# A long convolution with a spectral mix on one core: first-transform tiles of one sequence each, and the two real classes packed into one

## The chip, the cores and the metric

The kernel runs on one core of a Trainium2 chip. The metric is the device time of one launch in microseconds. The core has five instruction streams that run side by side and meet at semaphores: TensorE (PE), VectorE (DVE), ScalarE (ACT), GpSimd (POOL) and SyncE (SP). POOL and SP issue the DMAs here, SP without conversion, POOL also with conversion from float32 to float16.

## The reference

```python
# x: (8, 5696, 128), h: (5696, 128), w_r, w_i: (64, 128, 128), w_ch: (128, 128)
Xf = rfft(x, n=2 * S, axis=1); Hf = rfft(h, n=2 * S, axis=0)       # S = 5696
v = irfft(Xf * Hf[None], n=2 * S, axis=1)[:, :S]                   # causal convolution by channel
X = rfft(v, axis=1)                                                # length S
Y = zeros_like(X)
Y[:, :64] = X[:, :64] @ (w_r + 1j * w_i)                           # per mode, over channels
u = v + irfft(Y, n=S, axis=1)
out = u + maximum(u @ w_ch, 0)                                     # float32
```

## The kernel before

A position is s = 64 q + p, with q of 0 to 88 and p of 0 to 63. The padded transform of length 11392 is done in two steps. The *first transform* runs over q, as a matmul with the constant F (`f1_sb`): 89 values, padded to 178, give 90 *classes* k = 0 to 89, as pairs of real and imaginary columns, so 180 columns. The *second transform* runs over p within a class, as matmuls with the strip M (`m_sb`) of the class. Classes 0 and 89 are real after the first transform. Behind the product with the filter's spectrum Hs, matmuls with W1 and W2 (`wc_sb`) undo the second transform; the result Z goes to a scratch tensor in DRAM, and matmuls with G add up the 64 modes from it on chip. In the last stage (the tail) S4 undoes the first transform, the mixed modes are added, and output tiles are made.

The eight sequences go in four *pairs* (`g_`); a pair is 256 columns of 128 channels each, sequence `b` 0 and 1. The work of a pair is:

- **Placement** (`x_place`, DVE): eight pieces of x, four of each sequence (`XC`), are copied to Xin, in rows of 130 so that a matmul can read one channel of all 64 p. For pair 0 they come from Xr, loaded at the start by POOL's queue; for pair 1 from Xh and Xt, for later ones from Xt, loaded by POOL's queue once a buffer is free.
- **First-transform tiles** (`a_tile`, 32 in a pair): four matmuls of 180 columns, one for each of four channels. The stationary operand is Xin's channel for 64 p of *both* sequences, so partitions 0 to 63 of a result belong to sequence 0 and 64 to 127 to sequence 1. One eviction, on DVE or ACT, writes 128 x 720 to As. A tile needs all eight pieces.
- **Ticks** (`tick`, four classes each; 23 in a pair, the last with two classes): `second` makes 16 matmuls of 128 columns with a contraction over 64 rows; the result is copied by ACT to Xs (`copied`), or read from PSUM for some; DVE multiplies it with Hs in both partition halves to U (`products`); two ticks later (`LC`) four W matmuls of 512 columns and two ACT copies to Zs follow, and three ticks later (`LM`) the matmuls with G (`modes`).

Tick 0 has a way of its own, as it stands right behind the first-transform tiles: its second transform is done for the first 116 channels (120 in pair 0; `DA`, `DF`) ahead of the last tiles' evictions, then for the rest, and DVE makes three products of it (`first_u`: sequence 0 without the last channels, all of sequence 1 from ACT's copy, the last channels of sequence 0). For the other pairs, six tiles of the next pair run within the last ticks of the pair before (`border`), the other 26 behind it.

The filter h goes the same way at the start: 16 tiles from Hp, evicted to Ah, then *filter ticks* (`filter_tick`), six of them (`LH`) among the first-transform tiles of pair 0, the rest in pair 0's ticks, six ticks ahead of their use. A filter tick ends with a cast to Hs and two DMAs on SP's queue that write the copy with the partition halves swapped; a product needs cast and copies. Ah's place is then loaded with G.

At the start PE runs 92 filler matmuls, then the h tiles with four fillers behind each (but the last), then 22 long fillers (`LONG`), all into PSUM banks that nobody reads. The first-transform tiles of pair 0 go to DVE and ACT by a written list (`SHARE`). POOL issues the loads of h, then x of pair 0, then M in six parts, then Xh, each in the order of the code.

Every queue is in program order; the class `Recorder` adds the waits, from what each step reads and writes.

## Time and profile before

| | |
|---|---|
| median of three runs | 372.22 us (372.2 to 372.45) |
| span of the profiled execution, first to last instruction | 370.1 us |
| median less span | 2.1 us |
| mean granted clock of TensorE | 0.999 |
| bytes moved by DMA | 103.94 MB |

The page gives the profiled execution by its span; no time of that execution outside the span is listed. In the page's groups a line can be that of a helper: L323 is every matmul, L311, L313, L315 and L317 every eviction, L320 every DMA, so groups are told apart by the tiles: ps<-F,Xin is a first-transform tile, ps<-As,M a second transform, ps<-Ah,M a filter tick, ps<-U,Wc the W matmuls, ps<-G,Zs the modes. "128x720" is partitions by elements.

### The profile page before, as it was taken

To read this page: it belongs to the slowest core of one execution; us is meant where nothing else is said; L and a number is where in the kernel's file an instruction comes from. 1 tells how busy PE (TensorE), PEld (TensorE's weight loads), DVE (VectorE), ACT (ScalarE), POOL (GpSimd) and SP (SyncE) were. 2 spreads that over 40 slices of the span, in tenths; PEclk is the share of its full clock that TensorE was granted. 3 is DMA by queue.
4 is the path that set the end of the run, shared out by engine and by line. 5 is a ranking of instruction groups with operands and counts; after the bars stand their busy time and mean duration, and the time that the engine had idled before them with its cause. 6 is when DMAs were issued, how large, how long until landed. Compare 5 with 4: busy or idle time off the path is not lost.

```text
span 370.1 us, 12455 instructions
## 1 busy us (share of the span) xinstructions
PE 354.7 (96%) x5350; PEld 276.5 (75%) x5350; DVE 291.8 (79%) x332; ACT 316.2 (85%) x499; POOL 75.2 (20%) x117
## 2 busy tenths in 40 slices
PE   7999899999999999999999999999999999999994
PEld 7878766667866668866668766668899888888873
DVE  3549899988999999989999988775357777756666
ACT  8559999999999999999999999995467777688885
POOL 8804012100833311823213001151000000000000
PEclk9999999999999999999999999999999999999999
DMA  7999979969999996999996999999999999999878
GB/s 139 209 271 382 249 165 292 232 198 283 93 140 213 263 258 186 132 160 215 263 278 128 171 310 363 342 345 388 381 410 386 413 410 408 418 399 376 326 291 349
DMA packets 87048, 103.94 MB, mean 281 GB/s; under 512 B 22730, under 2 KB 72522, under 8 KB 83438
## 3 DMA queue, kind: packets, MB, share of 16 engines
q1 hardware_dynamic: 64610, 81.33, 62.5%
q0 software_dynamic: 22384, 21.83, 35.4%
q8 instruction: 42, 0.69, 0.7%
q14 instruction: 12, 0.10, 0.1%
HBM read 70.61 MB, written 51.12 MB: 329 GB/s over the span
## 4 chain that ended last, share of the span: by engine, by line
PE 78%; ACT 10%; DMA 7%; DVE 3%; issue 1%; POOL 1%; DVEq 0%; POOLq 0%
PE ps L323 78%; ACT As L313 6%; DMA out_dram<-O 5%; DMA Hin<-in_h_dram 2%; ACT R L898 1%; DVE As L317 1%; ACT Xs L311 1%; DVE U L623 1%; POOL Hin L320 1%; ACT UT L311 1%; DVE O L899 0%; ACT Zs L311 0%; DVE Hp L438 0%; ACT C L313 0%; DVE Hs L315 0%
## 5 line engine op out<-in xcount | busy, mean ns | idle before, releaser
L652 DVE TENSOR_TENSOR U<-Xs,Hs 128x2048 f16<-128x2048 f16 (+1 forms) x72 | 85.8, 1197 | 12.1 <-ACT Xs L311 11.5
L323 PE MATMUL ps<-U,Wc 128*128 128x512 f16 (+1 forms) x368 | 93.8, 376 | 1.4 <-DVE U L623 1.4
L311 ACT CAST Xs<-ps 128x1024 f16<-128x1024 f32 (+1 forms) x76 | 75.0, 995 | 5.8 <-PE ps L323 3.1
L311 ACT CAST Zs<-ps 128x512 f16<-128x512 f32 (+1 forms) x132 | 70.1, 605 | 0.7
L899 DVE TENSOR_TENSOR O<-ps,R 128x512 f32<-128x512 f32 x81 | 52.4, 684 | 21.6 <-ACT R L898 11.4
L898 ACT ACTIVATE R<-ps 128x512 f32<-128x512 f32 (+1 forms) x92 | 50.5, 592 | 8.5 <-PE ps L323 8.4
L317 DVE TENSOR_SCALAR As<-ps 128x720 f16<-128x720 f32 x64 | 53.1, 879 | 4.8 <-PE ps L323 3.3
L323 PE MATMUL ps<-As,M 64*128 64x128 f16 (+3 forms) x1504 | 52.5, 214 | 2.4 <-ACT As L313 1.2
L313 ACT ACTIVATE As<-ps 128x720 f16<-128x720 f32 (+1 forms) x68 | 48.2, 771 | 5.0 <-PE ps L323 4.8
L323 PE MATMUL ps<-F,Xin 128*128 128x180 f16 x512 | 52.1, 249 | 0.1
L323 PE MATMUL ps<-WI,UT 128*128 128x256 f16 x360 | 50.8, 278 | 0.5 <-ACT UT L311 0.4
L311 ACT CAST UT<-ps 128x712 f16<-128x712 f32 x46 | 34.5, 752 | 19.4 <-PE ps L323 18.4
L323 PEld LDWEIGHTS ps<-U,Wc 128*128 128x128 f16 x368 | 29.1, 97 | 28.2 <-DVE U L623 1.9
L323 PEld LDWEIGHTS ps<-F,Xin 128*128 128x128 f16 x512 | 45.2, 155 | 6.7 <-DVE Xin L365 0.9
L323 PEld LDWEIGHTS ps<-As,M 64*128 64x128 f16 x1504 | 42.2, 94 | 8.7 <-ACT Xs L311 1.9
L323 PEld LDWEIGHTS ps<-WI,UT 128*128 128x128 f16 x360 | 38.9, 152 | 3.2 <-issue 1.8
L323 PE MATMUL ps<-IBs,C 128*128 128x356 f16 x128 | 39.2, 314 | 0.8 <-DVE O L899 0.7
L320 POOL DMA_DIRECT2D Xt<-in_x_dram x40 | 21.4, 540 | 76.5 <-PE ps L323 76.0
L323 PEld LDWEIGHTS ps<-G,Zs 128*128 128x128 f16 x512 | 26.1, 96 | 14.1 <-ACT Zs L311 0.2
L652 DVE TENSOR_TENSOR U<-ps,Hs 128x2048 f16<-128x2048 f32 (+1 forms) x16 | 35.5, 2216 | 0.0
L323 PE MATMUL ps<-G,Zs 128*128 128x128 f16 (+2 forms) x512 | 31.9, 192 | 0.1
L311 ACT CAST Zt<-ps 128x512 f16<-128x512 f32 x52 | 29.1, 659 | 0.0
(76 smaller groups left out, 479.4 us busy)
## 6 DMA issues: line engine op xcount, KB each, us to landing
out_dram<-O SPq DMA_DIRECT2D x39, 512.0 KB, 10.5
zscr<-Zs SPq DMA_DIRECT2D x62, 256.0 KB, 6.7
zscr<-Zt SPq DMA_DIRECT2D x26, 256.0 KB, 6.6
Xt<-in_x_dram POOLq DMA_DIRECT2D x20, 320.0 KB, 6.9
W<-wscr SPq DMA_DIRECT2D x4, 1024.0 KB, 8.5
ZT0a<-zscr SPq DMA_DIRECT2D x4, 1024.0 KB, 11.0
M<-cM POOLq DMA_DIRECT2D x5, 720.0 KB, 17.6
ZT1a<-zscr SPq DMA_DIRECT2D x3, 1024.0 KB, 11.1
```

What stands on the lines that cost most here:

```text
L311: R.add(e, lambda h_: h_.copy(dst, src), reads, writes, after=after)
L313: R.add(e, lambda h_: h_.activation(dst, src, COPY, scale=scale), reads, writes, after=after)
L317: R.add(e, lambda h_: h_.tensor_scalar_mul(dst, src, scale), reads, writes, after=after)
L320: R.add(eng, lambda h_: h_.dma_start(dst, src), reads, writes, ring=ring, after=after)
L323: R.add("tensor", lambda h_: h_.matmul(o, l, r, start=st, stop=sp), reads, writes)
L623: R.add("vector", lambda e: e.tensor_tensor(bass.AP(u_s[0], b * 512 + d0, [[2048, P], [1024, 2], [D, n], [1, d1 - d0]]), bass.AP(s_[0], s_ ...
L652: R.add("vector", lambda e: e.tensor_tensor(uv, src, hv, MULT), bk + [("h", t, 0), ("h", t, 1, 0), ("h", t, 1, J)], [("u", i)])
L898: R.add("scalar", lambda e: e.activation(rv, src_r, RELU), bk, [("r", i % NR)], after=once(("r", i % NR), G_ALL + XTT + [("y", 0), ("y", 1 ...
L899: R.add("vector", lambda e: e.tensor_tensor(ov, src_u, rv, ADD), bk + [("r", i % NR)], [key + (h_,)], after=once(key, old))
```

## The change

- **Layout of tiles.** Xin is laid out by channel halves, in rows of 66. The stationary operand of a tile's matmul is now channel d and channel d + 64 of *one* sequence: tiles 0 to 15 are sequence 0, tiles 16 to 31 sequence 1, and partitions 64 to 127 hold the second half of the channels, as h's tiles had it before. The second transform, products, W matmuls and Zs copies follow this order: 64 channels of two sequences where there were 128 channels of one. Hs is kept per tick, plain and swapped half side by side.
- **Pair 0's start.** x is loaded sequence after sequence (12 DMAs instead of 14). Sequence 0's four pieces are placed among the h tiles; its tiles then run, and sequence 1's pieces are placed among them, after tiles 1, 5, 9 and 13. The filter ticks follow tiles 19, 21, 23, 25, 27 and 29 (before: 11, 14, ... 26). Xh's loads wait for the last placement as before. Two fillers stand behind each h tile instead of four, and four long ones instead of 22; six of the h evictions go to DVE instead of two; `SHARE` is rewritten.
- **Tick 0.** The second transform of sequence 0 stands behind the last tile on PE, that of sequence 1 waits for the last evictions. There are two products, one for each sequence. The slot `DA`/`DF` split is gone.
- **89 classes.** The real classes 0 and 89 are the real and imaginary part of one. F has 178 columns, a tile's eviction 712 elements, and the last tick one class. In tick 0 this class has weights of its own, V1 and V2, so its W matmuls are eight instead of four with as many columns; in `modes` it is a full class with 128 columns (class 89 was one before, class 0 had two). The scratch tensor keeps 90 classes, and one load fills the unused rows at the start of pair 1.

```diff
-    NK = NQ + 1
+    NK = NQ
...
+    for b_ in range(2):
+        for c_ in range(XC):
+            first_rows(b_, c_)
+            if c_ == 0:
+                next_rows(b_)
+                last_row(b_)
...
-    ZSLOT, DA, DF = 6, 116, 120
+    ZSLOT = (6, 4)
...
-    WARM, LONG = 92, 22
+    WARM, LONG = 92, 4
...
-        for i in range(4 if j < 15 else 0):
+        for i in range(2 if j < 15 else 0):
...
-             eng="vector" if j in (3, 7) else "scalar")
-        if j % 2:
-            i = j // 2 % 2 * XC + j // 4
-            x_place(i, bass.AP(x_all, i * XB, [[RA, NQ], [D, XN], [1, D]]), XR[i])
+             eng="vector" if j in (2, 4, 6, 9, 11, 14) else "scalar")
+        if j % 4 == 3:
+            i = j // 4
+            x_place(i, bass.AP(x_all, i * XB, [[RA, NQ], [D, XN], [DH, 2], [1, DH]]), XR[i])
...
-    def a_tile(j, slots, eng=None):
+    def a_tile(j, slots, eng=None, first_pair=False):
+        b_ = j // 16
+        xin = XIN[b_ * XC:b_ * XC + XC] if first_pair else XIN
...
-               ap(x_sb, XW, 0, P, d, [[XS, 2 * J]]), f1_sb[:, :], True, True,
-               XIN + XZ + [("f1",)], [bank(t + i // 2)])
+               ap(x_sb, XW, 0, P, d // DH * 2 * XH + d % DH, [[HS, 2 * J]]), f1_sb[:, :], True, True,
+               xin + XZ + [("f1",)], [bank(t + i // 2)])
...
+                for dh in range(2):
+                    col = m_col(k, r) + dh * J
+                    mm(pv(sl + dh, bs[0] * 256 + i * DH, [[256, nb], [1, DH]]),
+                       ap(m_sb, MW, J * dh, J, col, [[1, P]]),
+                       ap(a_sb, AW, J * dh, J, (2 * k + r) * D + bs[0] * DH, [[1, nb * DH]]), r == 0, r == 1,
+                       rd + mtok(k), [bank(sl + dh)])
...
+            product(g_, t, (ps, sl[0], 4096), bk[0], (0,))
+            second(g_, 0, (1,))
+            evac(bass.AP(x_s[e], 256, [[1024, P], [512, 2], [1, n]]), pv(ZSLOT[1], 256, [[512, 2], [1, n]]), bk[1], [("xs", e)], eng="scalar")
+            product(g_, t, (x_s[e], 0, 1024), [("xs", e)], (1,))
...
-                for r in range(2):
-                    mm(pv(zb[b], 0, [[1, n * D]]), (W1, W2)[r], u_s[i][:, r * 1024 + b * 512:r * 1024 + b * 512 + n * D],
-                       r == 0, r == 1, [("u", i), ("wc",)], [bank(zb[b])])
+                for lo, hi, w_ in ((0, DH, (V1, V2)), (DH, n * DH, (W1, W2))) if s_ == 0 else ((0, n * DH, (W1, W2)),):
+                    for r in range(2):
+                        mm(pv(zb[b], lo, [[n * DH, 2], [1, hi - lo]]), w_[r],
+                           ap(u_s[i], 2048, 0, P, r * 1024 + b * 512 + lo, [[256, 2], [1, hi - lo]]),
+                           r == 0, r == 1, [("u", i), ("wc",)], [bank(zb[b])])
...
-    SHARE = [V if c_ == "V" else A for c_ in "VAVAAVAVAVAVAVAVAVAAVVAVAVAVAVA"]
+    SHARE = [V if c_ == "V" else A for c_ in "VAAVAAVAAVAAVAAVVAVAVAVVAVAVAVA"]
+    HTICK = [19, 21, 23, 25, 27, 29]
     for j in range(32):
-        a_tile(j, FOUR, "both" if j == 31 else SHARE[j])
...
+        a_tile(j, FOUR, "both" if j == 31 else SHARE[j], True)
+        for i in range(NXH if j == 15 else 0):
+            x_load(1, i, x_h[i], xtok(i), [t_ for r_ in XR for t_ in r_])
+        if j in HTICK:
...
+            filter_tick(HTICK.index(j), [h_, h_ + 1])
+        if j % 4 == 1 and j < 16:
+            i = XC + j // 4
+            x_place(i, bass.AP(x_all, i * XB, [[RA, NQ], [D, XN], [DH, 2], [1, DH]]), XR[i])
+    second(0, 0, (0,))
```

## The prediction

> **What bounds the kernel now.** I read the page's busy shares first, then the chain of waits in order of time, then the timelines of the stretches that the change touches.

> ```profile
> span 370.1 us, 12455 instructions
> PE 354.7 (96%) x5350; PEld 276.5 (75%) x5350; DVE 291.8 (79%) x332; ACT 316.2 (85%) x499; POOL 75.2 (20%) x117
> ...
> 17.25 10.56 PE ps L323 x102
> ...
> 49.37 25.23 PE ps L323 x529
> 74.60 20.63 PE ps L323 x300
> 95.26 7.47 ACT As L313 x11
> 102.78 0.37 PE ps L323 x8
> 103.17 0.59 ACT Xs L311
> 103.78 0.70 DVE U L623
> 104.58 0.27 DVE U L623
> 104.90 43.31 PE ps L323 x644
> ```

> The busy shares say TensorE, but the chain shows three regimes. Inside a pair PE runs without a gap (43.31 us in one piece). At each border between pairs evictions of first-transform tiles take over (7.47 us), followed by a handover: eight small matmuls, a copy, two small products, then PE again at 104.90. The third regime is the start, where the 10.56 us of PE are mostly fillers that cover the loading of x. The change touches all three. The span is 370.1 us and the median of the runs 372.22, so 2.1 us lie around the span; I make the sum as a difference and take it off the median.

> **The start: what the engines could do.**

> ```profile
> 11.98 2.37 DVE L438 COPY Hp<-Hin 89x4096 f16<-89x4096 f16 x2 [6.71 <-DMA Hin<-in_h_dram]
> 23.22 4.27 PE L323 MATMUL ps<-Hp,F 128*128 128x344 f16 x22
> 26.33 0.69 DVE L365 COPY Xin<-Xr 89x2048 f16<-89x2048 f16 x1 [0.81 <-DMA Xr<-in_x_dram]
> 40.95 2.19 DVE L317 TENSOR_SCALAR As<-ps 128x720 f16<-128x720 f32 x3 [0.40 <-PE ps L323]
> 91.70 10.85 DVE L317 TENSOR_SCALAR As<-ps 128x720 f16<-128x720 f32 x13
> ```

> Before, no tile of x can start until the eighth piece is placed at 26.33 + 0.69 = 27.0 us, and the last eviction ends at 40.95 + 2.19 = 43.1. The change puts sequence 0's four pieces first. h had landed at 11.98 and all of x at 26.33, so half the bytes, in order, are there at about 11.98 + 14.35/2 = 19.2.

> DVE then sets the pace. It is free of the Hp copies at 14.35, and one eviction costs (10.85 - 0.45)/12 = 0.87 us (the thirteenth is a half tile). In its new order it has 6 Ah evictions and 4 placements: 14.35 + 0.4 for the first tile + 6 x 0.87 + 4 x 0.69 = 22.7. The x of sequence 0 is there 3 us before. Tiles of sequence 0 start then. Up to the placement of the eighth piece DVE has 5 evictions and 4 placements after half a microsecond of PE: 22.7 + 0.5 + 5 x 0.87 + 4 x 0.69 = 30.3, by which time sequence 1 (26.33) has long landed. The rest is 9 evictions, one Hs cast (0.68, a row of it below) and a half: 9 x 0.87 + 0.68 + 0.45 = 9.0, so 39.3. ACT, with 10 + 7.5 tiles at 7.47/11 = 0.68 and 5 casts, is done no later.

> So the evictions end 3.8 us earlier. The fillers taken out (30 of 180 columns; 18 of the 22 long ones, 18 x 0.194 = 3.5 us by the second row) are worth nothing by themselves: PE then waits for DVE, under a microsecond around 22.

> **The start: what becomes late next.** The first products need Hs in both partition halves, and the swapped half comes by a DMA of SP's queue.

> ```profile
> 12.12 4.90 POOL L320 DMA_DIRECT2D M<-cM  x6
> DMA to landing us min/median/max: 16.5/18.2/21.7
> 27.60 4.15 POOL L320 DMA_DIRECT2D Xh<-in_x_dram  x8 [10.58 <-DVE Xin L365]
> Xh<-in_x_dram POOLq DMA_DIRECT2D x4, 320.0 KB, 12.9
> L320 SPq DMA_DIRECT2D Hs<-Hs x2: 555/571/587, 33.0 to 33.6; - x2
> DMA to landing us min/median/max: 6.6/7.0/7.4
> L320 SPq DMA_DIRECT2D Hs<-Hs x2: 461/529/597, 36.8 to 37.3; - x2
> DMA to landing us min/median/max: 9.5/9.6/9.8
> L320 SPq DMA_DIRECT2D Hs<-Hs x2: 542/568/595, 48.5 to 49.0; - x2
> DMA to landing us min/median/max: 2.0/2.0/2.0
> 43.43 1.16 DVE L623 TENSOR_TENSOR U<-ps,Hs 128x960 f16<-128x960 f32 x1 [0.29 <-PE ps L323]
> 47.42 1.23 DVE L652 TENSOR_TENSOR U<-Xs,Hs 128x2048 f16<-128x2048 f16 x1 [0.51 <-ACT Xs L311]
> 48.57 0.68 DVE L315 CAST Hs<-ps 128x512 f16<-128x512 f32 x1
> ```

> A swap takes 2.0 us when the queues are quiet and 7 to 10 us behind M and Xh, whose last piece lands near 27.60 + 4.15 + 12.9 = 44.7. Tick 0's pair lands at 33.6 + 7.4 = 41.0, its product ran at 43.43: 2.4 us to spare. Tick 2's lands at 37.3 + 9.5 = 46.8 and its product ran at 47.42: only 0.6 to spare. In the changed kernel the filter ticks follow tiles 19, 21, ... 29. By the same DVE count tick 0's cast ends at about 33.5 and tick 2's at 36.5, so the swaps are issued within half a microsecond of the old times. The queue ahead is the same M and Xh: Xh's eight issues move behind the later last placement, 27.0 to about 31, but M is on its way until 38 (issued up to 17.0, landing 16.5 to 21.7 us after issue, the second row), so the transfers close up.

> Hence tick 2's product goes from 47.42 to about 46.8, not to the 43.6 that the evictions allow. What stands behind it on DVE in order is the Hs cast of 48.57, and the filter matmuls of the next tick wait for that bank; from there DVE has one product, one cast and every other tick a placement, against a PE that is as full, so nothing is won back. The start gives 47.42 - 46.8 = **0.6 us**. Its bounds are -1 (swaps a microsecond and a half later than now) and 3.8 (swaps land as issued on a quiet queue).

> **Each border, three times.**

> ```profile
> 142.06 0.60 PE L323 MATMUL ps<-U,Wc 128*128 128x256 f16 x4
> 142.50 0.53 PE L323 MATMUL ps<-F,Xin 128*128 128x180 f16 x4
> ...
> 144.47 0.33 PE L323 MATMUL ps<-G,Zs 128*128 128x4 f16 x4
> 144.68 10.17 PE L323 MATMUL ps<-F,Xin 128*128 128x180 f16 x104
> 51.88 0.61 PE L323 MATMUL ps<-As,M 64*128 64x128 f16 x16
> 52.43 1.04 PE L323 MATMUL ps<-U,Wc 128*128 128x512 f16 x4
> ```

> With 89 classes the 23rd tick holds one class instead of two. Its four W matmuls of 256 columns fill 142.50 - 142.06 = 0.44 us and half that at best; I take 0.20 saved. Its second transform loses four of eight matmuls at (52.43 - 51.88)/16 = 0.034: 0.13. Its mode matmuls halve from 144.68 - 144.47 = 0.21: 0.10, of which I count nothing at the border, since evictions bind there already. First-transform tiles shrink from 720 to 712 elements; at 0.87 us for 720 an upper bound is 0.01 us each, 0.10 over 13 evictions in a row.

> The handover loses its second small product, with the gap ahead of it: PE went on at 104.90, the product before it ended at 103.78 + 0.70 = 104.48, and a wake-up costs 0.05. That gives 0.37. Against it stand eight more small matmuls ahead of the Xs copy (0.05, since the eight of 102.78 take 0.37 and most of that is latency). Product 0 of sequence 0 grows from 928 to 1024 elements but runs while PE and ACT do sequence 1. In tick 2, class 0 has its own weights V1, V2: eight W matmuls instead of four with the same columns. No row shows that form; between 0 and four issues of 0.034 I take 0.05. Sum: 0.20 + 0.13 + 0.10 + 0.37 - 0.05 - 0.05 = **0.70**, between 0.3 (only the handover) and 0.9; three times, 2.1.

> The last pair has no border; its last tick, with the mode matmuls and two Zs copies of half the length on the path to the mix, gives 0.2 + 0.1 + 0.05 = **0.35**.

> **Edits at nothing.** Products, Zs copies and placements keep their element counts but run in pieces of 64 per class and sequence. Rows for short runs: As evictions move runs of two at 0.87 us for 720, Hp copies runs of 32, 4096 elements in 1.2 us. Neither is dearer per element than a contiguous run, so I put 0 and keep the opposite as a rival. The zpad load (one DMA on SP, waiting for nothing, in pair 1) and the two rows fewer in S4b are covered; no wait moves with them. The tail's loads are asked for by PE's progress, so the tail moves as a block.

> **Sum.** 0.6 + 2.1 + 0.35 = 3.05: 372.22 - 3.05 = **369.2 us**.

> **The rivals.**

> (a) The swaps do not bind, because they land as early as they are needed: the start gives 3.8 less 0.2, the total 6.0, time 366.2. For it: filter casts from tick 3 on come over a microsecond earlier than now. Against it: 9.5 us at a still loaded queue.

> (b) The swaps land up to 2 us later than now, as the casts slip behind a slower DVE sequence: 369.2 + 0.6 to 2.2, say 370.5. It decides from tick 2's landing at 47.4.

> (c) Nothing measurable: the swaps slip by 3 us and the start gives back what the borders save, 372.2. Chance small; the casts would have to come near 40.

> (d) Slower, on DVE: the new patterns halve its rate. The two rows are windows of the trace: length, busy time of PE, weight loads, DVE, ACT and POOL, granted clock, DMA share, GB/s.

> ```profile
> 104.90:143.70 38.80, 38.80 (x591) 25.66 (x592) 36.66 (x32) 37.76 (x63) 8.33 (x16) 1.00 1.06 230
> 27.30:42.80 15.50, 14.96 (x226) 12.78 (x224) 13.68 (x17) 14.02 (x22) 4.15 (x8) 1.00 1.04 329
> ```

> A placement of 0.69 us would then cost up to 1.38; with some of it fixed I take 1.2, which is 0.53 more. Eight of them before 39.3 make 4.2, of which the 3.2 by which the start outran the swaps are free; eight in pair 0, where DVE sets the pace, make 4.2; in each later pair 4.2 less DVE's idle 38.80 - 36.66 = 2.1 of the first row. Together 1.0 + 4.2 + 2 x 2.1 = 9.4: 378.6. It is slower than before once a placement costs 0.4 us more (8 x 0.4 in pair 0 alone eat the 3.05). The Hp row speaks against it.

> (e) Slower, on PE's clock: fillers go while PE sits idle between 14 and 48 us. In the second row the granted clock is 1.00 in the stretch where evictions set the pace and PE is fed below its rate, so such gaps have cost nothing so far. The longest that I expect is an estimate of 2.3 us, from about 46.3, when the matmuls behind tick 1's product are through, to 48.6, the end of the cast behind tick 2's. Were PE at half rate from 22 to the end of the stage, 128 tile matmuls at twice 10.17/104 = 0.098 us and 96 filter matmuls at twice 0.034 make 31.6 us as an upper bound; as the 0.098 is itself set by evictions I take 24. The evictions then end at 46.7 instead of 43.1, and 372.22 + 3.6 - 2.45 = 373.4. It is slower than before if they end after 45.6.

> [...]

> **How the numbers follow.** My sum has 0.50, (a) 0.18, (b) 0.12, (c) 0.08, (d) 0.06, (e) 0.06. The measurement can tell 0.2%, 0.74 us, from no change. Faster: the sum, (a) and (b), 0.80; same: (c), 0.08; slower: (d) and (e), 0.12. The range runs from (a) at 366.2 to 371.9: it takes in (b) and the lower bounds of the borders (3 x 0.4 less) and leaves out (c), (d) and (e).

> **What would show it.** Right: sequence 0's first tile near 22.7 us, the last eviction of the first stage near 39, product 0 waiting for an Hs DMA at about 41 and tick 2's product at about 46.8; each pair 0.7 us shorter from one handover to the next; one handover product fewer. Wrong: tick 2's product before 46 (then (a)) or after 47.4 ((b)); a placement or product slower than now ((d)); a clock below 1.00 between 14 and 48 us ((e)).

## The result: slower, 383.58 us, and the profile after

| | before | changed |
|---|---|---|
| median of 6 runs each, same chip | 372.34 us | 383.58 us (380.96 to 385.46) |
| ratio | | 1.0288, 95% interval 1.025 to 1.0326 |
| profiled execution, span | 370.1 us | 382.7 us |

The prediction said 369.2 us. The profiled execution of the changed kernel took 385.46 us, 1.9 above the median, so the losses read from it below add up to 12.6 us of span and not to the 11.2 of the medians. First the page of the changed kernel: busy shares, the clock in 40 slices of 9.6 us, and pieces of its chain (start, length).

```profile
PE 353.0 (92%) x5290; PEld 272.7 (71%) x5290; DVE 291.6 (76%) x331; ACT 312.7 (82%) x496; POOL 73.5 (19%) x115
PEclk9999989999999999999999999998899999999998
38.27 11.56 DMA Hs<-Hs
108.32 0.70 DVE U L657
239.93 8.71 DMA zscr<-Zt
249.51 7.07 DMA zscr<-Zs
```

No engine has more work than before, PE has 1.7 us less. The clock dips twice, near 50 and from 258 to 277 (means of 0.82 and 0.85 over these slices), and DMAs stand in the chain where before there was PE; three of them are shown. By *handover* I mean below the end of DVE's product of sequence 1 in tick 0 of a pair. Before, the three were at 104.47, 157.46 and 210.48; now they are at 109.01, 162.04 and 215.45. So 4.5 us are lost ahead of the first, 0.4 in pairs 1 and 2, and 7.7 between the third and the end (159.6 us before, 167.3 now). Two things about this measure. Before, a second small product follows the one that ends the handover, and PE goes on 0.42 us behind it (104.90); now it goes on 0.14 behind it (109.16), so handovers favour the kernel before by 0.28. And the first handover scatters: two kernels below whose start is the one of before had it at 104.47 and 105.49, and four with the changed start (two of them with 48 small matmuls more) at 107.34 to 109.01. A difference of 1 us in it, in single traces, shows nothing.

**Start.** DVE's timeline of the changed kernel (start, length, in brackets the idle time before):

```profile
23.65 0.90 DVE L341 TENSOR_SCALAR As<-ps 128x712 f16<-128x712 f32 x1 [0.63 <-PE ps L347]
29.58 0.68 DVE L389 COPY Xin<-Xr 89x2048 f16<-89x2048 f16 x1
38.52 1.62 DVE L341 TENSOR_SCALAR As<-ps 128x712 f16<-128x712 f32 x2 [0.25 <-PE ps L347]
42.90 1.22 DVE L657 TENSOR_TENSOR U<-ps,Hs 128x1024 f16<-128x1024 f32 x1 [2.76 <-DMA Hs<-Hs]
49.49 1.22 DVE L657 TENSOR_TENSOR U<-Xs,Hs 128x2048 f16<-128x2048 f16 x1 [3.21 <-DMA Hs<-Hs]
```

Evictions and placements come within a microsecond of the forecast; the products do not. Swaps on SP's queue, then PE, then two windows (length; busy of PE, weight loads, DVE, ACT, POOL; clock, DMA share, GB/s):

```profile
36.47 2.40 SPq L344 DMA_DIRECT2D Hs<-Hs  x4
38.91 0.59 SPq L344 DMA_DIRECT2D G<-cG  x1
40.55 4.90 SPq L344 DMA_DIRECT2D Hs<-Hs  x4
49.26 1.10 SPq L344 DMA_DIRECT2D Hs<-Hs  x2
DMA to landing us min/median/max: 12.4/12.6/12.7
51.37 0.41 PE L347 MATMUL ps<-Ah,M 64*128 64x64 f16 x16 [3.01 <-DVE Hs L339]
48.00:52.00 4.00, 0.99 (x38) 0.82 (x37) 2.51 (x4) 0.90 (x2) 0.00 (x0) 1.00 0.45 141
52.00:56.00 4.00, 4.00 (x55) 2.44 (x49) 4.00 (x5) 2.39 (x4) 1.04 (x2) 0.57 0.92 164
```

Tick 2's swaps, issued at 36.47, land 12.6 us later (9.6 before). The ring `"s"` has eight semaphores, so the ninth swap waits on SP for the first to land: four issues take 4.90 us instead of 2.40, and the next two stand until 49.26. PE stands 3.01 us, and the mean clock of the window from 52 to 56 is 0.57.

**Tail.** S4b is the second part of the constant S4, `zscr` the scratch tensor, Zs and Zt are the buffers from which Z is stored to it, and ZT0a and ZT0b the tail's first loads of Z. SP's queue around the load of S4b, the kernel before (two rows), the changed one (three), then ACT and PE of the changed one:

```profile
224.35 1.35 SPq L320 DMA_DIRECT2D S4b<-cS  x1
228.94 0.45 SPq L320 DMA_DIRECT2D ZT0b<-zscr  x1
...
228.59 0.42 SPq L344 DMA_DIRECT2D S4b<-cS  x1
229.85 2.62 SPq L344 DMA_DIRECT2D zscr<-Zt  x2
233.24 6.64 SPq L344 DMA_DIRECT2D ZT0b<-zscr  x1
...
249.75 1.07 ACT L335 CAST Zs<-ps 128x512 f16<-128x512 f32 x2 [2.15 <-DMA zscr<-Zs]
256.66 1.41 ACT L335 CAST Zs<-ps 128x512 f16<-128x512 f32 x4 [2.60 <-DMA zscr<-Zs]
257.30 0.34 PE L347 MATMUL ps<-U,Wc 128*128 128x128 f16 x2 [2.37 <-ACT Zs L335]
```

Behind an S4b of 82 rows the issue of ZT0b takes 6.64 us instead of 0.45, stores of Z land late, ACT waits for their buffers, and PE for ACT.

### The profile page after: what moved, and what is told of

Read it like the earlier page. It is cut to its first block, busy times and chain, and to the rows that moved or that the text cites. A ratio compares the mean times of both kernels' runs of the same rounds, so it can differ in the third digit from the quotient of the medians.

```text
span 382.7 us, 12323 instructions
## 1 busy us (share of the span) xinstructions
PE 353.0 (92%) x5290; PEld 272.7 (71%) x5290; DVE 291.6 (76%) x331; ACT 312.7 (82%) x496; POOL 73.5 (19%) x115
## 4 chain that ended last, share of the span: by engine, by line
PE 63%; DMA 15%; ACT 11%; DVE 5%; issue 3%; POOL 1%; SPq 1%; DVEq 0%; POOLq 0%; ACTq 0%
PE ps L347 62%; ACT As L337 8%; DMA Hs<-Hs 4%; DMA Xt<-in_x_dram 4%; DMA Xr<-in_x_dram 3%; DMA zscr<-Zt 2%; DMA zscr<-Zs 2%; DVE As L341 2%; DVE Xin L389 1%; ACT Xs L335 1%; ACT R L928 1%; POOL Hin L344 1%; ACT Zs L335 1%; DVE Hs L339 1%; DVE U L657 1%
## 5 line engine op out<-in xcount | busy, mean ns | idle before, releaser
L657 DVE TENSOR_TENSOR U<-Xs,Hs 128x2048 f16<-128x2048 f16 (+2 forms) x76 | 87.7, 1160 | 20.2 <-ACT Xs L335 11.3
L347 PE MATMUL ps<-U,Wc 128*128 128x512 f16 (+2 forms) x384 | 94.2, 367 | 7.3 <-ACT Zs L335 4.2
L335 ACT CAST Xs<-ps 128x1024 f16<-128x1024 f32 (+2 forms) x76 | 74.5, 988 | 12.9 <-PE ps L347 11.0
L341 DVE TENSOR_SCALAR As<-ps 128x712 f16<-128x712 f32 (+1 forms) x63 | 52.2, 873 | 5.3 <-PE ps L347 4.1
L347 PE MATMUL ps<-F,Xin 128*128 128x178 f16 x512 | 52.2, 249 | 1.9 <-DVE Xin L389 1.3
L347 PE MATMUL ps<-As,M 64*128 64x128 f16 (+1 forms) x1488 | 50.7, 215 | 2.3 <-ACT As L337 2.3
L337 ACT ACTIVATE As<-ps 128x712 f16<-128x712 f32 (+1 forms) x69 | 48.2, 764 | 3.8 <-PE ps L347 3.6
L347 PEld LDWEIGHTS ps<-As,M 64*128 64x128 f16 x1488 | 40.8, 95 | 7.5 <-ACT As L337 2.8
L657 DVE TENSOR_TENSOR U<-ps,Hs 128x2048 f16<-128x2048 f32 (+2 forms) x20 | 39.8, 1990 | 2.8 <-DMA Hs<-Hs 2.8
L347 PE MATMUL ps<-IBs,C 128*128 128x356 f16 x128 | 40.4, 325 | 0.1
L347 PE MATMUL ps<-G,Zs 128*128 128x128 f16 (+2 forms) x504 | 31.6, 194 | 0.2 <-ACT Zs L335 0.2
```

The lines of the kernel that those rows point to most:

```text
L335: R.add(e, lambda h_: h_.copy(dst, src), reads, writes, after=after)
L337: R.add(e, lambda h_: h_.activation(dst, src, COPY, scale=scale), reads, writes, after=after)
L341: R.add(e, lambda h_: h_.tensor_scalar_mul(dst, src, scale), reads, writes, after=after)
L347: R.add("tensor", lambda h_: h_.matmul(o, l, r, start=st, stop=sp), reads, writes)
L657: R.add("vector", lambda e: e.tensor_tensor(uv, sv, hv, MULT), bk + [("h", t, 0), ("h", t, 1, 0), ("h", t, 1, J)], [("u", i)])
```

## The experiments

Theory: S4b's 82 rows (tail) and the late swaps with their ring (start). Rivals: the fillers taken out; something else in the tail. All medians stand against the kernel before on the same chip (372.1 to 372.8 in the four sets); differences between kernels of different sets are taken as they stand, and can be off by these 0.7.

**S4b with 84 rows.**

```diff
-        n = PB + RB if part else P      # 82 rows
+        n = PB + RL if part else P      # 84 rows, the last two zero
```

> Changed kernel with one edit: the load of S4b takes 84 rows again (32 of padding, 50 of data, 2 rows of zeros) instead of 82. Theory (82 rows clog a few transfer engines, and the zscr stores, the ZT loads and the last Zs casts queue behind them, until PE's gaps drop its clock): the zscr stores issued near 229.9 and 231.8 land in about 7 us instead of 12 to 14, the 2.15 and 2.60 us of ACT idle near 249.8 and 256.7 go, the clock stays at 1.00 from 250 to 277, and the kernel takes 376 us, 7 to 8 less than the changed one (383.6). Rival (the tail is late for another reason, the longer rows of ZT0b or the zpad rows): the gaps stay, 383. Rival (the fillers taken out let the clock fall): no change in the tail, 383.

377.68 us, 1.0143 (1.0116 to 1.017), 5.9 less than the changed kernel. ZT0b's issue is short again, ACT's waits for stores are gone. It is 1.7 more than forecast: in the tail the clock still dips once (0.65 from 260 to 264), behind a gap that comes up below.

```profile
231.03 0.43 SPq L344 DMA_DIRECT2D ZT0b<-zscr  x1
```

**The reverse, in the kernel before:** the same bytes in two DMAs, of 82 and of 2 rows.

> Kernel before with one edit: S4b is loaded in two pieces, of 82 rows and of 2 rows, instead of one of 84. Theory: the same clog as in the changed kernel at the same place, so zscr stores behind it take over 12 us and the kernel goes from 372.2 to about 379 (plus 5 to 8). Rival (82 rows are covered, as the prediction had it): 372.2, within 0.3.

378.46 us, 1.0155 (1.012 to 1.0191): plus 5.8. The two runs agree, so the price of 82 rows is shown. The traces' packets tell how: S4b's 82 packets of 5874 bytes start between 231.2 and 242.1 in the changed kernel, never more than 10 in a microsecond, and the 84 of before between 227.0 and 231.1, 64 of them in the first two microseconds. Never more than 3 of the 82 are under way at once, here and in the kernel before with 82 rows; of the 84 it is up to 14 before, and up to 15 in the changed kernel with 84 rows. So of 82 rows about a fifth as many are under way at once as of 84; why two rows make this difference is not shown.

**A longer ring.** `("s", 8)` becomes `("s", 24)`.

> Changed kernel with one edit: the ring of semaphores for the swaps of Hs has 24 members instead of 8, so that a swap no longer waits on SP for the landing of the one eight before it. Theory (the ring blocks SP's queue from 40.6 to 49.3, and the swaps of ticks 4 to 13 stay late): swaps of tick 4 on are issued as their cast ends; the wait of 1.66 us for an Hs transfer at 74.9 goes; tick 2's product stays near 49.5, since its own transfer was issued at 36.5 and lands at 49.2; 381.5, 2 less than the changed kernel. Rival (the ring is not what is late, only the transfers' length is): 383.5.

381.56 us, 1.0258 (1.0211 to 1.0306): 2.0 less, as expected, but the interval overlaps that of the changed kernel (1.025 to 1.0326). The first handover comes at 106.38, 1.0 earlier than the earliest with the changed start. SP's wait is gone (the third four issues take 3.04 us); what that is worth in time is not clear of noise.

**The fillers of before.** `LONG` 22 again, four behind each h tile.

> Changed kernel with one edit: the filler matmuls of the start are as before (four a tile instead of two, 22 long ones instead of 4). Theory (fillers do not matter; what is late is the swaps and the tail's transfers): 383.6, within 0.5, with the clock still under 1.00 near 50 and near 260. Rival (without fillers the clock falls at the start and the loss comes from there): 374 or less.

378.9 us, 1.0177 (1.0152 to 1.0202): 4.7 less. My theory was wrong here: fillers matter. The clock near 50 is 1.00 now, as the long fillers hold back the first tiles by 3.8 us and PE's gap closes (busy for 3.58 us of the window from 48 to 52, instead of 0.99). The first handover (106.52) is 2.5 earlier than in the changed kernel's trace, more than half of it within the scatter, and the rest comes in the tail, 164.4 us instead of 167.3, which I could not explain yet.

**Xh later; dummies in PE's gap; ring and fillers; all three edits.** The four rest on S4b with 84 rows.

```diff
-        for i in range(NXH if j == 15 else 0):
-            x_load(1, i, x_h[i], xtok(i), [t_ for r_ in XR for t_ in r_])
+        for i in range(NXH if j == 29 else 0):
+            x_load(1, i, x_h[i], xtok(i), [t_ for r_ in XR for t_ in r_] + [("h", 2, 1, 0), ("h", 2, 1, J)])
```

> Changed kernel with S4b of 84 rows, and the four loads of Xh issued behind the landing of tick 2's swaps instead of behind tile 15. Theory (the swaps are late because Xh's bytes stand with M's in the transfer engines from 33 to 49): once M has landed at 39.3 the engines are empty, swaps of tick 0 land by 41 and of tick 2 by 42.5, tick 2's product runs by 45.5 instead of 49.5, PE's clock stays at 1.00, the first handover is near 103.5 instead of 107.5 to 109.2; 373.5, 4 less than with S4b alone (377.7). Rival (M and the swaps' own small rows make them late, Xh does not matter): swaps of tick 2 still land after 47, 377.5.

376.64 us, 1.0131 (1.0076 to 1.0186). Swaps of tick 2 land at 40.6 to 40.8 and its product runs at 45.19, so Xh is what made them late. The handover is at 105.83, 2.3 later than forecast, and the gain in time (1.0) is within the intervals.

```diff
+        for i in range({0: 8, 1: 8, 2: 16}.get(t, 0) if g_ == 0 else 0):
+            mm(pv(5, 0, [[1, 2 * NK]]), f1_sb[:, 0:P], f1_sb[:, :], True, True, [("f1",)], [bank(5)])
```

> Changed kernel with S4b of 84 rows, and 8, 8 and 16 dummy matmuls of 356 columns into a free bank at the end of ticks 0, 1 and 2 of the first pair; the transfers are untouched. It tells the wait apart from what the wait does to the clock. Theory (half of the start's loss is the clock, which falls to about 0.55 for 4 to 8 us behind PE's gap): tick 2's product stays at 49.5, the clock stays at 1.00 between 44 and 60, the first handover comes 1.5 to 2 us earlier than 107.5; 376. Rival (the wait itself is the whole loss): 377.7 or more, as the dummies take PE's time.

379.04 us, 1.0176 (1.0123 to 1.0229). The clock is 1.00 throughout the start:

```profile
48.00:52.00 4.00, 3.15 (x65) 2.09 (x63) 2.96 (x4) 2.17 (x4) 0.00 (x0) 1.00 0.49 145
52.00:56.00 4.00, 3.82 (x88) 2.61 (x86) 4.00 (x6) 3.66 (x6) 1.05 (x2) 1.00 0.86 174
```

and the handover is at 107.24, against 107.34 with 84 rows alone, whose clock was 0.54 and 0.61 in the windows from 44 to 52. So the gain of 1.5 to 2 us that the theory forecast is not there: at the start the wait is the loss, and no cost of the clock's fall on top of it shows. (A dummy has 178 columns in this code, not the 356 that the expectation names.)

> Changed kernel with S4b of 84 rows, 24 semaphores for the swaps, and the fillers as before. The long fillers hold back the first tiles by 3.8 us, so that the evictions end near 44 as before and PE has no gap before the swaps land. Theory (what costs is PE standing still with the evictions done, and the ring behind it): the first handover near 105.5, 373.5. Rival (ring and fillers mend the same loss, so together they bring no more than one): 106.7, 374.5.

372.65 us, 1.0019 (0.9995 to 1.0042), no different from before. The handover is at 107.02, later than either theory had it, and no earlier than with the fillers and the ring of eight (106.52); the tail takes 157.7.

> Changed kernel with S4b of 84 rows, 24 semaphores for the swaps, and Xh behind tick 2's swaps; fillers as changed. Theory (with the swaps in time the early end of the evictions counts at last): product 0 at 41 to 42, tick 2's product by 45.5, first handover near 102 to 103, 370.5, a little less than before (372.5). Rival (the tail is bound by its transfers, whose engines are full from 215 on, so an earlier start is lost there): the handovers come 2 us earlier than before and the end does not, 372.5.

376.99 us, 1.0131 (1.0082 to 1.0179). Product and handover (44.77 and 104.36) come as early as I could wish, and the end does not. DVE in pair 0, and PE in the tail:

```profile
44.77 1.23 DVE L657 TENSOR_TENSOR U<-Xs,Hs 128x2048 f16<-128x2048 f16 x1 [0.50 <-ACT Xs L335]
DVE U L657 <- DMA Hs<-Hs: 3.5, 4, 1.1
257.81 0.28 PE L347 MATMUL ps<-XT,W 128*128 128x32 f16 x4 [2.74 <-issue]
256.00:260.00 4.00, 1.97 (x24) 1.80 (x25) 0.69 (x1) 0.42 (x1) 0.00 (x0) 0.65 1.04 392
260.00:264.00 4.00, 4.00 (x33) 2.84 (x31) 2.09 (x3) 1.58 (x3) 0.00 (x0) 0.50 1.02 366
```

Two things show. Tick 2's product is 2.7 us earlier than before, but four waits for later swaps (3.5 us in all) give it back in pair 0. And PE stands 2.74 us in the middle of the mix's matmuls (ps<-XT,W, which apply the weights of the 64 modes, with matmuls of S4 between them), put down to "issue": it waits for no engine. The same gap is in the runs with 84 rows alone, with Xh later and with dummies; in the last, with 32 matmuls more ahead of it, it comes after 108 matmuls of the stretch instead of 140. A place that moves with the count of instructions points to how they are fetched. The trace has packets of 16384 bytes of the kind "instruction" (*blocks* below). In the kernel before there are 42 of them, and from the start of the first to that of the last 10492 matmuls and weight loads of TensorE start: 256 a block. Their starts near the mix:

```
before              239.88  249.84  256.60  262.66     no gap
all three edits     244.09  255.43  262.11             PE stands 255.07 to 257.81
```

The packet that ends the gap starts when PE has already run dry. So a new theory: the 48 fillers taken out (of 60 matmuls fewer in all) move the ends of these blocks against the code, and one now stands behind 140 matmuls of the mix that pass in 4.4 us, while the DMA share is 1.11 (248 to 252) and 1.04 (252 to 256).

The traces settle where the gap stands. In the changed kernel (1.38 us) and with 84 rows, Xh later, dummies and all three edits (2.74 to 2.79), exactly 7617 instructions of TensorE that the trace records (matmuls, weight loads, entries of its queue) start ahead of it, whatever code is there. In four of these five a second gap, of 0.7 to 1.0 us between 292 and 300, stands 1024 or 1280 instructions further on, four or five times 256. Each time PE goes on 2.3 to 2.5 us after the packet's start. Why the packet starts so late is open: with all three edits it starts 4.46 us after the mark 256 instructions earlier, in the kernel before 3.51, where these 256 take 6.1 us instead of 4.1.

**48 matmuls without work**, ahead of the first h tile, with S4b of 84 rows; then the same with all three edits; then fewer fillers in the kernel before.

```diff
+    for i in range(48):
+        mm(pv(6 + i % 2, 0, [[1, 4]]), f1_sb[:, 0:P], f1_sb[:, 0:4], True, True, [("f1",)], [bank(6 + i % 2)])
```

> Changed kernel with S4b of 84 rows, and 48 matmuls of 4 columns more ahead of the first h tile, where TensorE idles for 1.1 us. They do no work; they move every later instruction of TensorE by 96 places (a weight load and a matmul each) against the blocks of 16384 bytes in which its instructions are fetched. Theory (in the kernels without the 48 fillers a block ends in the 140 short matmuls of the mix near 252, its successor comes only at about 257, TensorE stands 2.7 us and its clock falls): no stall of 2.7 us near 256, from the last handover to the end about 158 us instead of 161.7, 374. The fillers of the fourth run would then have helped in two ways, by holding back the first tiles and by this shift. Rival (the stall comes of the late transfers alone): 377.7.

373.21 us, 1.0012 (0.9989 to 1.0036): 4.5 less than without the 48, with the first handover no earlier (107.52 and 107.34). The tail takes 158.9; a gap of 1.0 is left in place of 2.8, behind the same 7617 instructions, which are now 92 matmuls into the mix.

> Changed kernel with S4b of 84 rows, 24 semaphores, Xh behind tick 2's swaps, and the 48 small matmuls ahead. Theory of the instruction blocks: first handover near 104.4 as without the 48, from the last handover to the end 158 instead of 163, 371.8. Rival (late transfers alone): 377.

372.2 us, 0.9982 (0.9952 to 1.0012): 4.8 less. The gap is gone. The tail takes 161.2, not 158, with two loads of ZT late by 0.76 and 1.00; the profiled execution is the longest of ten (373.71). PE's waits from 46 to 260, with all three edits, without and with the 48 (sum, times, longest):

```profile
PE ps L347 <- issue: 2.7, 1, 2.7
PE ps L881 <- issue: 0.2, 1, 0.2
...
PE ps L883 <- issue: 0.5, 1, 0.5
```

> Kernel before with the fillers of the changed kernel (two a tile instead of four, 4 long ones instead of 22), nothing else. Prediction's view (fillers are worth nothing by themselves; x lands at 26.3 and sets the start): 372.3, within 0.5. Theory of the instruction blocks: 48 matmuls fewer put the end of a block into the mix near 250, a stall of 2 to 3 us and a fall of the clock there, 375 to 377. Rival (TensorE, idle from 18 to 27, falls to a lower clock before the first tiles): the loss lies ahead of 45 us, 374.

377.15 us, 1.0116 (1.008 to 1.0152): 4.4 more than the kernel before, by leaving out matmuls that nobody reads. PE from 225 to 262:

```profile
PE ps L323 <- issue: 3.0, 2, 2.8
27.00:37.00 10.00, 9.88 (x129) 8.89 (x128) 8.06 (x10) 8.00 (x12) 4.16 (x8) 0.83 1.03 379
```

The gap is there, behind 7617 instructions again, and the tail 2.3 longer (161.9). The second row is the last rival's: the clock falls to 0.83 from 27 to 37, and the first handover is 1.1 later (105.53). But the kernel before with S4b in two pieces had it at 105.49 with all its fillers, so a loss at the start is not shown. The split of the 4.4 is not settled to better than that, as an Xt is late by 1.4 in pair 2 too.

**Is it one loss or two?** The 48 matmuls alone, S4b at 82 rows.

> Changed kernel with the 48 small matmuls ahead and nothing else; S4b keeps its 82 rows. Theory (two separate losses): the waits for zscr stores near 250 and 257 stay, since they are not a matter of instructions, and the block ends at another place: 379.5 to 381, 2.5 to 4 less than the changed kernel (383.6). Rival (one loss, the block's end, set off by the late transfers): 374.

379.2 us, 1.0167 (1.0136 to 1.0197): 4.4 less than the changed kernel. With 84 rows alone 5.9, both 10.4: two separate losses that add up. The waits for stores stay, as expected, and the time is 0.3 below the theory's range. Of the 4.4 to 4.8 us that the 48 matmuls are worth in the three pairs of kernels, 3.3 to 3.9 lie in the span (medians) and the rest outside it: the time of a run less its span is 1.8 to 1.9 us in every run of the kernel before in the four sets and of the kernels with its fillers or the 48 matmuls, and 2.5 to 3.1 in 14 of the 22 runs of the changed kernel and its variants with 84 rows, the long ring, Xh later or all three edits. What passes there is not shown.

**What paces pair 0.** All three edits and the 48, and `XLATE` [6, 9, 12, 15] instead of [3, 6, 9, 12]; then also `XPLACE[0]` [5, 7, 9, 11, 13, 16, 19, 21].

> As the run before it, and the four loads of Xt in the first pair are asked for at ticks 6, 9, 12 and 15 instead of 3, 6, 9 and 12. Theory (pair 0 is paced by its transfers, whose engines are full from 44 to 76 and not after it, so an earlier start is given back in five waits for swaps of 0.4 to 1.1 us): two or three of these waits go, the first handover comes near 102.5, 370. Rival (the waits for swaps come of the swaps' own number): 104.4 again, 372, or later if the last Xt comes late for its placement.

370.95 us, 0.9926 (0.9901 to 0.9952). This is the first version that beats the kernel before. But the handover is at 105.35, not 102.5, and was at 105.06 without this edit: the waits of products for swaps fall from 3.5 to 0.8 us, but one for Xh has come, 1.92 us up to 48.36, so pair 0 gains nothing. In the traces what is gained lies in the tail, 157.4 against 161.2.

> As the eleventh run, and the placements of pair 1's eight pieces stand at ticks 5, 7, 9, 11, 13, 16, 19 and 21 of pair 0 instead of 3, 5, 7, 9, 11, 14, 17 and 20. Theory (VectorE waits at 46.4 for an Xh that is asked for late, and the products queue behind it): that wait goes, TensorE is full from 44 to 80, the first handover comes near 103.5 instead of 105.4, 369.5. Rival (pair 0 is paced by the sum of its transfers, whatever stands first): handover at 105 again, 371.

370.38 us, 0.995 (0.9922 to 0.9979). That wait goes, and the next swap is late (issued at 44.82, landed at 55.20). The profile puts the product's wait down to ACT's copy to Zs, which the product does not read; the swap is what it reads:

```profile
55.28 1.23 DVE L659 TENSOR_TENSOR U<-Xs,Hs 128x2048 f16<-128x2048 f16 x1 [2.54 <-ACT Zs L335]
52.00:60.00 8.00, 5.86 (x94) 3.46 (x93) 5.46 (x8) 5.23 (x8) 1.29 (x2) 0.85 1.08 307
```

Handover at 104.95. So the rival fits: in three orders of the transfers the wait moves and the handover stays (105.06, 105.35, 104.95). That the sum of the transfers sets it is argued from this, and no run takes bytes away. The last two versions are not told apart (370.95 and 370.38); both are 0.5 to 0.7 per cent faster than before.

## Why the prediction was wrong

The loss of 11.2 us is 5.9 (S4b) and 4.4 (what the 48 small matmuls take off, in the span and outside it), which add to 10.3. With both mended the kernel is not told apart from the kernel before (1.0012, 0.9989 to 1.0036): what borders and tail give, the start takes.

- **"the two rows fewer in S4b are covered"** is the costliest step that failed. I looked for who waits for the two rows, and not for what an 82-row DMA does to the queue: 5.9 us instead of 0.
- **"The fillers taken out ... are worth nothing by themselves"** failed: 4.4 us. I asked what stands in their place at 22 us; what the traces show of the price was at 255 to 300.
- **Start, +0.6.** The engine steps held: first eviction of a tile of x at 23.65 (tiles from 22.7), eighth placement done at 30.26 (30.3), DVE's last eviction done at 40.14 (39.3). The step "the transfers close up" failed: Xh moved behind M ran beside the swaps, which landed 12.6 us after issue, so tick 2's product came at 49.49 instead of 46.8 (the bound was "a microsecond and a half later"; it was 2.1 later than before). Instead of 0.6 gained, the first handover came 1.9 to 4.5 us later. The ring of eight I had not looked at; the long one took 2.0 off, not clear of noise. And rival (a) would not have given its 6.0: with swaps in time the handover was at 104.36 and 105.06, not told apart from the kernels with the start of before (104.47 and 105.49).
- **Borders, 0.70 each.** The handover gave 0.28 of its 0.37. In a run with no late transfer in pair 1 a pair takes 52.82 from handover to handover, 52.99 before: 0.17. The last tick gave nothing: from the last long product on a PSUM bank to the first border eviction 141.97 - 135.59 = 6.38, before 141.52 - 135.13 = 6.39. And PE's going on earlier only moved the wait to the next product, which stands on ACT's copy:

```profile
135.59 2.28 DVE L659 TENSOR_TENSOR U<-ps,Hs 128x2048 f16<-128x2048 f32 x1
141.97 1.71 DVE L341 TENSOR_SCALAR As<-ps 128x712 f16<-128x712 f32 x2 [0.30 <-PE ps L347]
157.19 0.69 DVE L659 TENSOR_TENSOR U<-Xs,Hs 128x1024 f16<-128x1024 f16 x1 [0.18 <-ACT Xs L335]
158.11 2.36 DVE L659 TENSOR_TENSOR U<-Xs,Hs 128x2048 f16<-128x2048 f16 x2 [0.23 <-ACT Xs L335]
```

- **Last pair, 0.35; "the tail moves as a block".** The 0.35 is not too much: without the gap, the clog and late ZT loads the tail takes 157.4 to 157.7 in three runs, 1.9 to 2.2 less than before (0.28 of it by where the handover is taken). The block did not hold: its loads and stores came late behind the 82 rows, and a gap of PE's, behind 7617 of its instructions, stands in it.
- **Rival (d)** is refuted: a placement takes 0.68 us (0.69 before), product and Zs copy 1.22 and 0.62 as before. **Rival (e)**: the clock did fall (0.57), but behind the late swaps, and no price of it showed there (the run with dummies). The gap estimated at 2.3 us was one of 3.01, and no run shows a length of gap up to which the clock holds: those of 3.01 and 2.74 us were followed by windows of four microseconds with mean clocks of 0.57 and 0.50.

## What to carry to other kernels

Before changing the number of rows of a DMA, look at what queues behind it, not only at who reads it: here two rows fewer took the packets under way from 14 or 15 to 3 and cost 5.8 and 5.9 us. Before dropping or adding instructions that do no work, look for gaps that wait for no engine: here 48 such matmuls were worth 4.4 to 4.8 us, and the gap of 2.74 us stood behind 140 small matmuls that passed in 4.4 us at a DMA share of 1.04 to 1.11. Follow a gain to the next handover before counting it: here a product that came 2.7 us earlier was followed by four waits for swaps of 3.5 us in all.
